# The last wait of a decode kernel: ahead of SyncE's final branch, or behind it

## The chip, the cores and the metric

The kernel runs on one core of a Trainium2 chip. The metric is the device time of one execution in microseconds (us). The profile lists the instructions of five engines apart: TensorE, called PE; VectorE, called DVE; ScalarE, called ACT; GpSimd, called POOL; SyncE, called SP. A "q" behind an engine's name in the profile (SPq) means its sequencer: waits, branches and issues of transfers. The profile's span runs from the first to the last instruction of the program; a little of the timed execution comes after it, and this case is about that part (in the profiled run of the kernel before, 1286.23 us were timed and the span is 1284.81 us).

"Landing" means here the last update that a finished transfer makes to its semaphore.

## The reference

One decode step: layer norm of a row `x` of 640 numbers, attention over a cache of 32 heads, 32,768 positions and 128 numbers per position, and beside it a SwiGLU block; both are added to `x`.

```python
def _A_ref(x, k_cache, v_cache, wq, wo):
    ...
    scores = jnp.einsum("bhqd,bhkd->bhqk", q, k) * (Dh ** -0.5)
    p = _softmax(scores, axis=-1)
    o = jnp.einsum("bhqk,bhkd->bhqd", p, v)
    return (...)(o, 0, 2, 1, 3).reshape(B, Sq, Hq * Dh) @ wo

def _B_ref(x, w_gate, w_up, w_down):
    return (_silu(x @ w_gate) * (x @ w_up)) @ w_down

xn = _layernorm(x, axis=-1)
return x + _A_ref(xn, ...) + _B_ref(xn, ...)
```

The K and V caches are bfloat16, 268 MB each. The output is one row of 640 bfloat16 numbers.

## The kernel before

SyncE issues nearly all transfers, in the order in which buffers come free. At the end it waits for the output row, issues the store, and waits until the store has landed. Each engine's function lies in a block; when the block closes, each engine gets a branch to a common final block. The kernel empties that final block, so nothing of the program follows the branch.

```python
        block = es.enter_context(nc.Block(no_gpsimd_drain=True))
        ...
            @block.sync
            def sp(e):
                ...                                   # K, V and weight loads
                e.wait_ge(s_fin, 2)                   # the output row is there
                e.dma_start(out[0, 0:1, :].rearrange("o (r m) -> (o r) m", m=32),
                            orow[:, :]).then_inc(s_out, 16)
                e.wait_ge(s_out, 16)                  # the store has landed
        ...
            @block.vector
            def dve(v):
                ...
                v.wait_ge(s_or, 1)
                v.tensor_copy(out=orow[:, :], in_=orow_ps).then_inc(s_fin, 1)

    nc.main_func.blocks[-1].instructions = []         # behind the exit from the block
```

Of the kernel before, what the change touches and what calls it, by code (L numbers as in the profile page):

```python
# [12 lines left out]
def bass_parallel_sum__gqa_block_cached__swiglu_ffn__decode_kernel(  # L13
# [66 lines left out]
    with ExitStack() as es:  # L80
# [3 lines left out]
        def sem(name):  # L84
            return es.enter_context(nc.semaphore(name))
# [34 lines left out]
        s_x, s_wq, s_out = sem("x"), sem("wq"), sem("o")  # L120
# [26 lines left out]
        def ahead(start):  # L147

            at_start = nc.main_func.blocks[0]
            n = len(at_start.instructions)  # L150
            start()
            ins = list(at_start.instructions)
            new = ins[n:]
            drain = next(i for i, x in enumerate(ins)
                         if x.engine == new[0].engine and type(x).__name__ == "InstDrain")
            at_start.instructions = ins[:drain] + new + ins[drain:n]

        ahead(lambda: nc.sync.dma_start(wq, A_wq.rearrange("(p c) n -> p (c n)", c=NCD)).then_inc(s_wq, 16))
        ahead(lambda: nc.scalar.dma_start(xrow, A_x[0, 0:1, :]).then_inc(s_x, 16))
        block = es.enter_context(nc.Block(no_gpsimd_drain=True))  # L160
        f0 = FFN_S * CE
        wg = flat[:, f0:f0 + NCD * F]
        wu = flat[:, f0 + NCD * F:f0 + 2 * NCD * F]
# [22 lines left out]
        def kv_src(cache, h, j0, n):  # L186
            return cache[0, h].rearrange("(p j) d -> p (j d)", p=128)[:, j0 * DH:(j0 + n) * DH]
# [20 lines left out]
        with nc.psum_tensor("ps8", [128, 8, 512], F32) as ps8:  # L208
# [11 lines left out]
            @block.sync  # L220
            def sp(e):
                owner = {}
                for u in units:
                    s = slot_of[u]
                    if s in owner:
                        e.wait_ge(*owner.pop(s))
                    if u[0] == "wq":
                        owner[s] = (s_q, NQB)
                    elif u[0] == "k":
                        e.dma_start(ring[:, s, :], kv_src(A_k_cache, u[1], 0, NJ)).then_inc(s_slot[s], 16)  # L230
                        owner[s] = (s_qk, NHF * (u[1] + 1))
                    elif u == LASTV:
                        j = 0
                        for i, n in enumerate(TAIL):
                            e.dma_start(ring[:, s, j * DH:(j + n) * DH],
                                        kv_src(A_v_cache, u[1], j, n)).then_inc(s_tail[i], 16)
                            j += n
                    elif u[0] == "v":
                        e.dma_start(ring[:, s, :], kv_src(A_v_cache, u[1], 0, NJ)).then_inc(s_slot[s], 16)
                        owner[s] = (s_pv, u[1] + 1)  # L240
                    elif u[0] == "ffn":
                        e.dma_start(wg, B_w_gate.rearrange("(p c) n -> p (c n)", c=NCD)).then_inc(s_ffn[0], 16)
                        e.dma_start(wu, B_w_up.rearrange("(p c) n -> p (c n)", c=NCD)).then_inc(s_ffn[1], 16)
                        e.dma_start(flat[:, d0:d0 + FM * D], B_w_down[0:FM * 128, :].rearrange(
                            "(p j) n -> p (j n)", j=FM)).then_inc(s_ffn[2], 16)
                        e.dma_start(wdr, B_w_down[FM * 128:F, :].rearrange(
                            "f (t n) -> (f t) n", t=2)).then_inc(s_ffn[2], 16)
                    else:
                        wo_src = A_wo.rearrange("(p j) n -> p (j n)", j=OC)
                        j = 0  # L250
                        for i, n in enumerate(WTAIL):
                            e.dma_start(wo[:, j * D:(j + n) * D], wo_src[:, j * D:(j + n) * D]).then_inc(s_wo[i], 16)  # L252
                            j += n
                e.wait_ge(s_fin, 2)
                e.dma_start(out[0, 0:1, :].rearrange("o (r m) -> (o r) m", m=32), orow[:, :]).then_inc(s_out, 16)
                e.wait_ge(s_out, 16)

            @block.gpsimd
            def pool(g):
# [383 lines left out]
                v.wait_ge(s_or, 1)  # L643
                v.tensor_copy(out=orow[:, :], in_=orow_ps).then_inc(s_fin, 1)

    nc.main_func.blocks[-1].instructions = []


# [26 lines left out]
```

## Time and profile before

| what | value |
|---|---|
| time, median of the first three runs | 1286.45 us (1286.17 to 1286.59) |
| span | 1284.8 us |
| mean transfer rate over the span | 431 GB/s |
| issue of the output store | 1283.50 us |
| landing of the store | 1284.756 us |
| end of the span | 1284.806 us |
| last update of the closing sequence | 1286.344 us |

The last four lines are counted from the span's start. The last landing and the last update come from the trace's records of semaphore updates, to the nanosecond; none of the views lists these. The semaphore of the store has eleven updates there: one 0.50 us after the start of its issue, then ten, 13 to 14 ns apart, the last of them at 1284.756.

First the page of the kernel before: its span, the transfers in 40 slices of it in tenths, and the shares of the chain that ended last.

```profile
span 1284.8 us, 10032 instructions
...
DMA  9999999999999999999999999999999999999998
...
DMA 53%; PE 29%; DVE 11%; issue 6%; DVEq 0%; SPq 0%
```

The transfer engines are busy for 9 tenths or more in 39 of the 40 slices; only the last falls below. With 554.16 MB moved at a mean of 431 GB/s, and 51% of the chain that ended last in transfers of K alone, the stream of K and V sets the time.

The timeline of the kernel before, from 1282.5 us (start, duration, engine, line, operation, output<-inputs; in brackets the idle time before it and what ended it):

```profile
1282.82 0.18 DVE L641 TENSOR_TENSOR outb<-ps,blk 128x20 bf16<-128x20 f32 x1 [11.11 <-PE ps L451]
...
1283.06 0.20 PE L476 MATMUL ps<-fold,outb 128*20 128x32 bf16 x1 [0.27 <-DVE outb L641]
1283.29 0.18 DVE L644 CAST orow<-ps 20x32 bf16<-20x32 f32 x1 [0.29 <-PE ps L476]
1283.50 0.39 SPq L255 DMA_DIRECT2D out_dram<-orow  x1
```

Then the waits of SyncE's queue (line that waited <- what it waited for: us in total, times, longest), and the view of the source line 80:

```profile
SPq L80 <- DMA out_dram<-orow: 0.9, 1, 0.9
```

```profile
L80 POOLq COMPARE_BRANCH  x1: 33/33/33, 4.5 to 4.5; - x1
L80 SPq COMPARE_BRANCH  x1: 33/33/33, 1284.8 to 1284.8; - x1
```

The wait for the store was written on line 256, but the profile has it on line 80, which is the `with` statement whose exit closes the block. The compiler let the branch itself carry the wait. So the order on SyncE is: issue the store, 0.9 us of waiting, then a branch of 33 ns, with which the span ends.

What follows is not in the views, but its traces are in the record of semaphore updates. Semaphore 2 has four updates from 1283.431 to 1283.622 us, which I put down to the other engines. Its next update comes at 1285.024, 218 ns after the branch; I take it for SyncE's, since SyncE is the only engine that is late. Then 226 other semaphores have one update each, from 1285.158 to 1285.755, and semaphore 2 has its last at 1286.344. I read this as a closing barrier, a reset of the semaphores and a second barrier, and call it so; the records show the updates and not their purpose, nor what puts them in. From SyncE's update to the last one it takes 1.32 us.

### The profile page before, as it was taken

The numbers are of one execution on the slowest core, as the hardware profiler recorded it, in microseconds if no ns is written. First come the engines' busy times: TensorE is split into PE (matmuls) and PEld (weight loads), VectorE is DVE, ScalarE is ACT, GpSimd is POOL, SyncE is SP. The second block draws the span as 40 slices with busy tenths as digits, with TensorE's granted clock in tenths as the row PEclk, the third lists the DMA queues.
The fourth block names the chain that finished last, engine by engine and source line by source line (L and its number), as shares of the span: only waits on it lengthen the run. The fifth ranks groups of instructions, "written<-read, shape, count | busy, mean of one in ns | idle before, by whom it ended". The sixth has DMA issues, their size and how long they took to land.

```text
span 1284.8 us, 10032 instructions
## 1 busy us (share of the span) xinstructions
PE 1043.2 (81%) x5160; PEld 261.3 (20%) x3240; DVE 672.2 (52%) x409; ACT 52.2 (4%) x139; POOL 2.6 (0%) x18
## 2 busy tenths in 40 slices
PE   3599777789777788778898887798788798778897
PEld 1021112221112221112221112221112221112227
DVE  0855665445664446664446664446654446654451
ACT  2000000000000000000000000000000000000000
POOL 0000000000000000000000000000000000000000
PEclk9799888898888999888998888998888998888995
DMA  9999999999999999999999999999999999999998
GB/s 424 424 453 425 426 427 445 428 433 441 431 433 426 445 428 433 439 433 426 433 445 428 431 431 441 428 433 445 428 431 426 445 428 433 439 433 431 428 429 368
DMA packets 10987, 554.16 MB, mean 431 GB/s; under 512 B 1247, under 2 KB 1504, under 8 KB 1760
## 3 DMA queue, kind: packets, MB, share of 16 engines
q1 hardware_dynamic: 10974, 554.00, 99.8%
q8 instruction: 9, 0.15, 0.0%
q14 instruction: 2, 0.02, 0.0%
q10 hardware_dynamic: 2, 0.00, 0.0%
HBM read 553.99 MB, written 0.00 MB: 431 GB/s over the span
## 4 chain that ended last, share of the span: by engine, by line
DMA 53%; PE 29%; DVE 11%; issue 6%; DVEq 0%; SPq 0%
DMA ring<-in_A_k_cache_dram 51%; PE ps L358 16%; DVE ring L577 11%; PE ps L310 10%; DMA ring<-in_A_wo_dram 2%; PE ps L342 1%; PE ps L329 1%; PE ps L400 0%; PE ps L394 0%; PE ps L388 0%; PE ps L451 0%; SPq L252 0%; DVEq L577 0%; DVE sc L583 0%; DVE pmax L589 0%
## 5 line engine op out<-in xcount | busy, mean ns | idle before, releaser
L577 DVE TENSOR_TENSOR ring<-ring,qb 128x8192 bf16<-128x8192 bf16 x128 | 557.8, 4420 | 314.8 <-DMA ring<-in_A_k_cache_dram 314.8
L310 PE MATMUL ps<-ring,ident 128*128 128x512 bf16 x1920 | 498.9, 419 | 0.0
L358 PE MATMUL ps<-ring,P 128*4 128x512 bf16 x1920 | 429.0, 379 | 0.0
L329 PE MATMUL ps<-ring,ident 128*128 128x512 bf16 x128 | 55.9, 437 | 218.7 <-DVE ring L577 218.2
L358 PEld LDWEIGHTS ps<-ring,P 128*4 128x4 bf16 x1920 | 158.1, 85 | 230.1
L329 PEld LDWEIGHTS ps<-ring,ident 128*128 128x128 bf16 x128 | 12.6, 99 | 616.9 <-issue 313.3
L583 DVE TENSOR_REDUCE sc<-ps 128x64 f32<-128x512 f32 x128 | 82.3, 684 | 63.8 <-PE ps L310 63.8
L595 DVE TENSOR_SCALAR negb<-ps 128x1 f32<-128x1 f32 x32 | 5.1, 159 | 108.4 <-PE ps L400 108.4
L503 ACT ACTIVATE P<-sc,negb 128x256 bf16<-128x256 f32 x32 | 16.2, 508 | 956.9 <-DVE negb L595 956.9
L592 DVE TENSOR_REDUCE m<-ps 1x1 f32<-1x128 f32 x32 | 8.9, 278 | 85.2 <-PE ps L394 85.2
L380 PEld LDWEIGHTS ps<-identf,o 4*128 4x128 f32 x248 | 30.7, 190 | 13.1 <-issue 13.1
L380 PE MATMUL ps<-identf,o 4*128 4x1 f32 x248 | 33.3, 251 | 0.0
L388 PEld LDWEIGHTS ps<-rsum,ones 128*128 128x128 f32 x64 | 12.1, 190 | 99.9 <-issue 99.1
L494 ACT ACTIVATE o<-ps,rzb 4x512 f32<-4x512 f32 x31 | 21.0, 678 | 6.3 <-PE ps L345 6.3
L301 PE MATMUL ps<-ring 128*128 x40 | 11.1, 448 | 10.6 <-DMA ring<-in_A_wq_dram 10.6
L499 ACT ACTIVATE ocol<-ps 128x1 f32 (+1 forms) x31 | 5.4, 174 | 222.3 <-PE ps L380 222.3
L342 PE MATMUL ps<-ring,P 128*4 x64 | 14.4, 379 | 0.0
L589 DVE TENSOR_REDUCE pmax<-sc 128x1 f32<-128x256 f32 x32 | 13.4, 420 | 0.0
L394 PE MATMUL ps<-identf,pmax 128*1 128x128 f32 x64 | 12.2, 272 | 1.2 <-DVE pmax L589 1.2
L400 PE MATMUL ps<-m,ones 1*128 1x1 f32 x64 | 12.1, 256 | 0.4 <-DVE m L592 0.4
L400 PEld LDWEIGHTS ps<-m,ones 1*128 1x128 f32 x64 | 9.4, 182 | 14.0 <-issue 13.3
L565 DVE RECIPROCAL rzb<-ps 128x1 f32<-128x1 f32 x32 | 5.1, 158 | 8.1 <-PE ps L388 8.1
(75 smaller groups left out, 97.4 us busy)
## 6 DMA issues: line engine op xcount, KB each, us to landing
ring<-in_A_v_cache_dram SPq DMA_DIRECT2D x2, 4096.0 KB, 36.3
ring<-in_A_wq_dram SPq DMA_DIRECT2D x1, 5120.0 KB, 15.0
ring<-in_A_wo_dram SPq DMA_DIRECT2D x3, 1280.0 KB, 24.2
ring<-in_B_w_gate_dram SPq DMA_DIRECT2D x1, 2160.0 KB, 22.6
ring<-in_B_w_up_dram SPq DMA_DIRECT2D x1, 2160.0 KB, 27.5
ring<-in_B_w_down_dram SPq DMA_DIRECT2D x1, 2080.0 KB, 30.9
ring<-in_A_wo_dram SPq DMA_DIRECT2D x1, 800.0 KB, 28.3
ring<-in_A_k_cache_dram SPq DMA_DIRECT2D x32, 41.4
```

The lines of the kernel that those rows point to most:

```text
L310: return t.add_instruction(mybir.InstMatmult(start_tensor_calc=False, stop_tensor_calc=stop, tile_size=(128, 128), tile_position=(0, 0), l ...
L329: t.matmul(ob, lhsT=ident[:, :], rhs=src, start=True, stop=False)
L342: t.matmul(O, lhsT=P[:, h % PR, bass.ds(b * (RUN * W) + j, W)], rhs=flat[:, bass.ds(b * (RUN * W * DH) + (s * CE + j * DH), W * DH)], star ...
L358: mm = t.matmul(O, lhsT=P[:, h % PR, j:j + W], rhs=ring[:, s, j * DH:(j + W) * DH], start=(j == 0), stop=(j + W == NJ))
L380: mm = t.matmul(fold_ps, lhsT=o4[:, m * DH:(m + 1) * DH], rhs=identf[0:W, m:m + 1], start=(m == 0), stop=(m == W - 1))
L394: t.matmul(misc[0:1, 0:128], lhsT=pmax[:, h % SR:h % SR + 1], rhs=identf[:, :], start=True, stop=True).then_inc(s_t, 1)
L400: t.matmul(misc[:, 128:129], lhsT=ones[0:1, :], rhs=m1[0:1, h % SR:h % SR + 1], start=True, stop=True).then_inc(s_b, 1)
L494: a.activation(out=o4[:, :], in_=O, func=ACTF.Copy, scale=rzb[0:W, h % SR:h % SR + 1]).then_inc(s_o4, 1)
L503: a.activation(out=P[:, h % PR, :], in_=sc[:, :], func=ACTF.Exp, bias=negb[:, h % SR:h % SR + 1], scale=c_scale, accum_out=rsum[:, h % SR: ...
L577: v.tensor_tensor(out=kh, in0=kh, in1=q[:, None, :].to_broadcast([128, HF, DH]), op=ALU.mult).then_inc(s_mul, 1)
L583: v.tensor_reduce(out=sc[:, i * HF:(i + 1) * HF], in_=bank[i].rearrange("p (j e) -> p j e", e=G), axis=AX.X, op=ALU.add).then_inc(s_red, 1)
L589: v.tensor_reduce(out=pmax[:, h % SR:h % SR + 1], in_=sc[:, :], axis=AX.X, op=ALU.max).then_inc(s_max, 1)
```

## The change

The intent: the branch (33 ns in the view above) costs time behind the landing, where nothing hides it. Taken first, it would run while the store is under way, and only the bare wait would be left for the end.

```diff
-        block = es.enter_context(nc.Block(no_gpsimd_drain=True))
+        body = ExitStack()
+        block = body.enter_context(nc.Block(no_gpsimd_drain=True))
...
                 e.dma_start(out[0, 0:1, :]..., orow[:, :]).then_inc(s_out, 16)
-                e.wait_ge(s_out, 16)
...
-    nc.main_func.blocks[-1].instructions = []
+        body.close()
+        nc.main_func.blocks[-1].instructions = []
+        nc.sync.wait_ge(s_out, 16)
```

## The prediction

> **What bounds the kernel.** The page of the profile gives a span of 1284.8 us, a DMA share of 9 tenths in 39 of 40 slices and a mean of 431 GB/s. The chain that ended last is 53% DMA and 29% PE. Nearly all of the time is the stream of K and V from HBM; the change does not touch it.
>
> **Where the change acts.** It acts after the last compute. The timeline's last entry is SyncE issuing the output store at 1283.50 us (0.39 us). The waits of the SyncE queue list one wait of 0.9 us for the store's landing, on the source line of the block's end: the view of that line shows one COMPARE_BRANCH of 33 ns on SyncE (start 1284.773), which carries the wait. So the order now is: issue, wait for landing, branch, end. The span ends with this branch, at 1284.806. The trace also records semaphore updates after it: 218 ns pass until SyncE's update of the closing barrier (1285.024), and the last closing update is at 1286.34, near the profiled run's 1286.23 us. So a closing sequence of about 1.5 us seems to be in the timed 1286.45 us, and it starts only when SyncE is through its branch. The other four engines had updated that barrier by 1283.62.
>
> **What the change removes, adds and moves.** It moves the branch into the 0.9 us in which SyncE waits anyway, and adds one bare semaphore wait in the final block (17 ns on SyncE elsewhere in the trace). The landing, 1.27 us from issue to wait's end, stays.
>
> What comes off the critical path is the branch (33 ns against 17 ns) and the restart of SyncE's instruction stream at the branch target, which has no record. Estimates: a taken loop branch on PE takes 208 ns, a not taken one 76 ns: 132 ns. From its last completed work to a barrier update PE needed about 160 ns and DVE about 140 ns; SyncE needed 268 ns from the landing's last recorded update (1284.756). The difference is about 0.1 us. [...] 218 ns leave no room for one, since instruction fetches in this trace take about 1 us per 16 KB packet. So I expect no saving of a microsecond.
>
> **Sum.** The gain is about 0.1 us (0.05 to 0.2), 0.01% of the time, under the 0.42 us spread of the three runs before. Predicted: 1286.35 us, range 1285.8 to 1286.8. Chances: faster by over 2% 0.002, within 2% 0.996, slower by over 2% 0.002.
>
> **What would show it right.** SyncE's wait for the store stays at about 0.9 us but on a semaphore instruction that ends the span; the COMPARE_BRANCH with the wait is gone; the span shortens by about 0.02 us or drowns in noise; SyncE's barrier update follows the landing by about 0.15 us, not 0.27; everything before 1283.5 us is the same.
>
> **What would make it wrong.** The runtime's ending waits for something else, so nothing starts earlier; the branch target needs a fetch that collides with the store; or the HBM stream differs between runs by more than the effect, which is likely at this size.

What is cut from it, for the reading of its sum: it came to a gain of about 0.1 us, so 1286.45 less 0.1 = 1286.35 us, and no term of that is gone. Cut are a figure for the time of a branch, which I had set beside the 0.1 us as a check, and a statement on when a branch waits for a fetch of instructions; no run here shows either. In what is left, "no room for one" means room for such a fetch. The "restart" of the stream was an assumption of mine with a size estimated from this trace, and "the runtime's ending" is my name for the closing sequence; neither is shown as such.

## The result, and the profile after

| | before | after |
|---|---|---|
| time, median of 4 runs each | 1286.36 us (1286.17 to 1286.59) | 1286.26 us (1286.17 to 1286.32) |
| ratio of after to before, 95% interval | | 0.9999 (0.9982 to 1.0016) |
| span of the profiled run | 1284.806 us | 1284.897 us |
| issue of the store | 1283.499 us | 1283.606 us |
| landing to SyncE's update of the barrier | 268 ns | 197 ns |
| landing to the last closing update | 1588 ns | 1515 ns |

A ratio is the mean time of one kernel's fast runs over that of the other's from the same rounds, so it isn't quite the ratio of the medians. By time alone the two kernels are the same. The last two lines show the effect of the change: 71 ns come off between the landing and the barrier, and they arrive at the end (73 ns).

The span of the changed kernel is 0.09 us longer, though its ending is shorter. In this execution the store was issued 0.107 us later; that comes from the stream ahead of it, not from the change: the matmuls on the last weights (line 451) already began 0.09 us later (1281.43 against 1281.34 us). The page, the timeline, the waits and the view of the last source line, of the kernel after:

```profile
span 1284.9 us, 10032 instructions
...
DMA  9999999999999999999999999999999999999998
```

```profile
1283.40 0.18 DVE L644 CAST orow<-ps 20x32 bf16<-20x32 f32 x1 [0.29 <-PE ps L476]
1283.61 0.39 SPq L256 DMA_DIRECT2D out_dram<-orow  x1
```

```profile
SPq L648 <- DMA out_dram<-orow: 0.9, 1, 0.9
```

```profile
L648 SPq EVENT_SEMAPHORE  x1: 17/17/17, 1284.9 to 1284.9; - x1
```

The wait is as long as before, 0.9 us, but a semaphore instruction of 17 ns carries it now, on the line that the change added. The trace has no SyncE branch in the block's exit any more.

Is it only unrecorded, or not there? The end of SyncE's compiled program settles it (one line per instruction; labels are marks for branch targets):

```text
before: DMA store | COMPARE_BRANCH, waits for the store | 19 labels
after:  DMA store | 19 labels | EVENT_SEMAPHORE, waits for the store
```

The compiled kernel before has 9 COMPARE_BRANCH instructions in all, the kernel after has 8. (Listing and counts are of the compiled programs; no view of the profile has them.) The final block follows directly in SyncE's program, so a branch to it with nothing to wait for does nothing, and the compiler drops it. **The change did not move the branch into the waiting time; it made it vanish.** The words of the change describe a program that was not built.

### The profile page after: what moved, and what is told of

The parts are those of the page before. It is cut to its first block, busy times and chain, and to the rows that moved or that the text cites. A ratio compares the mean times of both kernels' runs of the same rounds, so it can differ in the third digit from the quotient of the medians.

```text
span 1284.9 us, 10032 instructions
## 1 busy us (share of the span) xinstructions
PE 1042.9 (81%) x5160; PEld 261.2 (20%) x3240; DVE 672.2 (52%) x409; ACT 52.1 (4%) x139; POOL 2.6 (0%) x18
## 4 chain that ended last, share of the span: by engine, by line
DMA 53%; PE 29%; DVE 12%; issue 5%; SPq 0%; DVEq 0%
DMA ring<-in_A_k_cache_dram 51%; PE ps L358 16%; DVE ring L577 12%; PE ps L310 10%; DMA ring<-in_A_wo_dram 2%; PE ps L342 1%; PE ps L329 1%; PE ps L400 0%; PE ps L394 0%; PE ps L388 0%; PE ps L451 0%; SPq L253 0%; DVEq L577 0%; DVE sc L583 0%; DVE pmax L589 0%
```

## The experiments

All kernels gave correct results. "Landing to barrier" is read as above: from the last update of the store's semaphore to SyncE's update of the barrier. Every change described as "against after" or "against before" starts from that kernel. All clocks were 0.887 to 0.890, as before.

| run | what SyncE does behind the store's issue | landing to barrier, ns | landing to last update, ns |
|---|---|---|---|
| before, before_again | branch that carries the wait | 268, 268 | 1588, 1588 |
| after, after_again | wait alone | 197, 197 | 1515, 1514 |
| branch_ahead | branch, then wait | 201 | 1520 |
| wait_in_block | wait (in its old place), no branch | 213 | 1532 |
| wait_then_branch | wait, then branch | 378 | 1697 |
| hops_ahead6 | 7 branches, then wait | 742 | 2060 |
| sems_after | wait, 31 semaphore instructions | 2296 | 3609 |
| hops_after | wait on the first of 32 branches | 4775 | 6090 |
| far_after | wait on a far branch | 2606 | 4010 |
| far_ahead | far branch, then wait | 2041 | 3359 |

### before_again: is the 268 ns a property of the program?

No edit.

> The kernel before, profiled a second time. Measured: the interval from the last recorded update of the store's semaphore to SyncE's update of the closing barrier (semaphore 2), 268 ns in the first profile of before and 197 ns in that of after. If the 71 ns are an effect of the program, this run shows 268 ns within about 10 ns. If they are noise of one execution, it may show anything from 190 to 280 ns.

Measured: 268 ns, and 1588 ns to the end, both equal to the first profile to the nanosecond. This interval repeats far better than the time: the issue of the store, which the stream of K and V sets, lay between 1283.435 and 1283.876 us over all twelve profiles, 0.44 us apart. The difference of 71 ns is therefore a property of the program and not noise.

### branch_ahead: the change as its words have it

```diff
# against after
                 e.dma_start(out[0, 0:1, :]..., orow[:, :]).then_inc(s_out, 16)
+                e.wait_ge(s_fin, 2)      # already met; the branch carries it and is kept
```

> The change as its words say it: in the compiled program of after SyncE has no branch left at all, so here the branch gets a wait that is already met and is therefore kept, ahead of the wait for the store. Theory R (a taken branch behind the landing costs its 33 ns and a restart of the stream): a COMPARE_BRANCH is recorded before the landing and the interval landing to barrier is 197 ns, as in after. Rival D (only the missing branch helps, one branch less anywhere): the interval is near 268 ns.

The view of the two lines in question, of this run:

```profile
L647 SPq COMPARE_BRANCH  x1: 33/33/33, 1284.2 to 1284.2; - x1
```

```profile
L649 SPq EVENT_SEMAPHORE  x1: 17/17/17, 1284.7 to 1284.7; - x1
```

The branch is there and is taken at 1284.214 us, 0.48 us ahead of the landing at 1284.698. Landing to barrier is 201 ns. A branch that is really taken first is as good as none, to within 4 ns. Rival D, by which only a missing branch helps, falls.

### wait_in_block: does the place in the source matter?

```diff
# against before
                 e.wait_ge(s_out, 16)
+                e.sem_inc(s_fin, 1)      # this instruction carries the wait, so the branch doesn't
```

> The wait stays in the engine's own block, ahead of the branch in the source, but a semaphore instruction carries it, so that the compiler drops the branch. Theory R: 197 ns from landing to barrier, as in after, since no branch follows the landing. Rival P (it matters that the wait stands in the final block): 268 ns, as before.

Measured: 213 ns. The 16 ns above 197 lie behind the wait: in both runs the instruction that waits ends 34 ns after the landing, and the barrier update follows 179 ns later here, 163 ns in after. Two things differ there, the added count and the place of the 19 labels, which lie behind the wait here; this run does not separate them. The wait stands where it stood in the kernel before, and 55 of the 71 ns are still gained. So neither the final block nor the separate context for the block is needed; it is enough that no branch follows the landing. Rival P falls.

### wait_then_branch: is it the branch, or the wait that it carries?

```diff
# against before
                 e.wait_ge(s_out, 16)
+                e.sem_inc(s_fin, 1)
+                e.wait_ge(s_fin, 2)      # already met; the branch carries it
```

> A semaphore instruction carries the wait for the store, and a branch with a wait that is already met follows it. Theory R: the branch and its restart are still behind the landing: 268 ns plus about 17 ns for the added instruction, so 270 to 300 ns. Rival C (a wait that a branch carries is answered later than one on a semaphore instruction, and a branch itself is cheap): 197 ns plus 17 to 33 ns, so 215 to 235 ns.

Measured: 378 ns, outside both expectations. The record shows why: the wait ends 34 ns after the landing and the branch begins only 92 ns later. I had counted 17 ns for one more instruction and left out the gap between two instructions of SyncE; together, 109 ns, they make up the 110 ns by which 378 exceeds 268. The question itself is answered by what follows the branch: 219 ns from its end to the barrier, against 218 ns in the kernel before. A branch that waits and one that doesn't are followed by the same gap, and it is 55 ns longer than the 163 ns behind a bare wait. Rival C also had a wait on a branch answered late; but the branch of before starts 17 ns after the landing, and so does the semaphore instruction of after. Rival C falls.

So the 71 ns are accounted for: 16 ns because a branch takes 33 ns where the bare wait takes 17, and 55 ns because the barrier update comes later behind the branch (218 ns) than behind the bare wait (163 ns). That SyncE's stream resumes later because the branch is taken is theory R's name for these 55 ns. No run has a branch in this place that is not taken, so it is not shown whether the jump or the branch instruction as such costs them. They are no wait for a fetch: the last instruction fetch started 114 ns after SyncE's update in before and 126 ns ahead of it in before_again, where it was still under way at the update, and the interval was 268 ns both times.

### hops_after and sems_after: thirty-two times as much

```diff
# hops_after, against before
                 e.wait_ge(s_out, 16)
+                for n in range(32):
+                    e.wait_ge(s_fin, 2)          # already met
+                    e.br(f"hop{n}")
+                    nc.switch_bb(f"hop{n}")

# sems_after, against before
                 e.wait_ge(s_out, 16)
+                e.sem_inc(s_fin, 1)
+                for n in range(31):
+                    e.wait_ge(s_fin, 2)          # already met
+                    e.sem_inc(s_fin, 1)
```

> 32 taken branches behind the landing in place of 1 (each carries a wait that is already met, so that it is kept; each goes to the next instruction). Measured so far: one more semaphore instruction behind the landing cost 110 ns (378 against 268), and a branch in its place cost 71 ns more than a semaphore instruction (268 against 197). Theory R (a taken branch costs a restart of the stream): each hop takes about 110 + 71 = 180 ns, so the interval landing to barrier is about 268 + 31 x 180 = 5.8 us (4.5 to 7), the time rises by about 5.6 us, and hops_after is about 2.2 us slower than sems_after. Rival S (every SyncE instruction costs the same and a branch has no cost of its own): about 31 x 110 = 3.4 us more, the same as in sems_after.

> The control of hops_after: 32 semaphore instructions behind the landing (the first carries the wait for the store, the others waits that are already met; each also counts one semaphore up), and no branch. Both theories: about 31 x 110 = 3.4 us more than the 213 ns of the run with one such instruction, so 3.6 us (2 to 4). Theory R: about 2.2 us less than hops_after; rival S: the same as hops_after.

The time was 1290.83 us for hops_after and 1288.23 us for sems_after, with 1286.27 us for the kernel before in the same rounds; ratios 1.0036 (1.0019 to 1.0052) and 1.0015 (0.9998 to 1.0032). The two groups in the view of their line, one fence for each run:

```profile
L259 SPq COMPARE_BRANCH  x32: 32/33/33, 1284.9 to 1289.4; - x32
```

```profile
L260 SPq EVENT_SEMAPHORE  x31: 17/17/17, 1285.0 to 1287.0; - x31
```

Thirty-two branches take 4.5 us from the first to the last, and 31 semaphore instructions 2.0 us. In the records the steady step is 145 ns from branch to branch and about 67 ns from one semaphore instruction to the next. A taken branch therefore costs 78 ns more than a semaphore instruction, near the 71 ns of the change. (Behind the last of each chain the barrier update follows 203 and 133 ns later, both less than behind a single instruction, but again 70 ns apart.) The step of both was smaller than I expected (180 and 110 ns), because I had taken the gap behind the first wait, 92 ns, for the steady one, which is 50 ns. The difference that separates the theories is 2.6 us in time (1290.83 less 1288.23) and 2.48 us from landing to barrier (4775 less 2296), against 2.2 expected by theory R and none by rival S. Rival S falls.

These runs also show that the timed execution contains what follows the span. The times rose by 4.56 and 1.96 us over the kernel before; the interval from landing to last update rose by 4.50 (6090 less 1588) and 2.02 us (3609 less 1588). In far_after, below, most of the added time is outside the span: the profiled run took 1288.98 us, with a span of 1285.1 us.

### hops_ahead6: how much fits ahead of the landing

```diff
# against after
                 e.dma_start(out[0, 0:1, :]..., orow[:, :]).then_inc(s_out, 16)
+                for n in range(6):
+                    e.wait_ge(s_fin, 2)
+                    e.br(f"hop{n}")
+                    nc.switch_bb(f"hop{n}")
+                e.wait_ge(s_fin, 2)
```

> Seven taken branches ahead of the wait for the store, which stands in the final block. Measured so far: 145 ns from one such branch to the next, and the first of them started 0.39 us after the end of the store's issue, 0.48 us ahead of the landing. So three of them are hidden and the seventh ends 0.39 + 6 x 0.145 + 0.03 = 1.3 us after the issue's end, 0.42 us after the landing, and the wait itself some 0.1 us later. If hiding ends where the landing wait ends, the interval landing to barrier is 0.6 to 0.8 us. If any number of branches ahead of the wait were free, it would be 197 ns.

```profile
L259 SPq COMPARE_BRANCH  x6: 33/33/33, 1284.3 to 1285.0; - x6
```

Six of the branches are in this group, the seventh follows at 1285.187; the store had landed at 1284.777. The interval is 742 ns, within the expectation. Work ahead of the wait is free only until the landing. The room was smaller than the 0.9 us wait of the profile: with a wait (already met) right behind the issue, the first branch began 0.40 us after the issue had ended (0.39 us in branch_ahead).

### far_after and far_ahead: a target 1024 instructions away

```diff
# both: a test that is never true jumps over 1024 instructions
+                zero_r = e.alloc_register("never")   # at the start of SyncE's function
+                e.reg_mov(zero_r, 0)
...
                 # far_after: e.wait_ge(s_out, 16) stands here; far_ahead: only in the final block
+                with e.If_ne(zero_r, 0):
+                    for _ in range(1024):
+                        e.sem_inc(s_fin, 1)
```

> The branch that carries the wait for the store now jumps over 1024 instructions that are never run[...]. Theory F (a branch to code that is not fetched waits for a fetch): the interval landing to barrier grows from 268 ns by about 0.8 us, to 0.7 to 1.6 us, and an instruction fetch starts after the branch; the last fetch in the profiles of before and after took 0.3 to 0.5 us for its data alone. Rival (targets cost the same near or far): 268 ns.

> The same jump over 1024 instructions, but ahead of the wait, which stands in the final block: what the change's words describe, with a branch that really is there. In the run with a kept branch SyncE took that branch 0.48 us ahead of the landing. If a fetch takes 0.8 us from there, 0.3 us of it are left behind the landing: an interval of 0.2 to 0.6 us, and 0.4 to 0.6 us less than far_after, in the timed runs too. If the fetch starts earlier or is shorter: 197 ns, all hidden. If position doesn't matter: as far_after.

Measured: 1288.80 us for far_after and 1287.99 us for far_ahead, against 1286.27 us for the kernel before; ratios 1.0019 (1.0002 to 1.0036) and 1.0013 (0.9996 to 1.0029). The branch of far_ahead and the wait behind it, in the views of their lines:

```profile
L259 SPq COMPARE_BRANCH  x1: 45/45/45, 1284.0 to 1284.0; - x1
```

```profile
L653 SPq EVENT_SEMAPHORE  x1: 17/17/17, 1286.7 to 1286.7; - x1
```

The branch ends at 1284.062 us and the next instruction starts at 1286.708: 2.65 us for one jump. The store had landed at 1284.828, so 0.77 us of the jump were hidden and the rest was not. In far_after all of it lies behind the landing: 2544 ns from the branch's end to the barrier, against 218 ns for the near branch. The rival (near or far cost the same) falls. Theory F fits as far as a fetch does follow the jump; that the jump waits for it is not shown, and both sizes were wrong: for far_after I expected 0.8 us and the jump adds 2.34 us (2606 less 268); for far_ahead I expected an interval of 0.2 to 0.6 us and it is 2.04. I had only the transfer of the instructions to go by (0.3 to 0.5 us), and the 0.8 us of a fetch was an estimate. In the trace the fetch that follows the jump starts 0.87 us after the branch and takes 0.40 us (0.87 and 0.57 us in far_ahead); what the rest of the 2.5 us consists of the trace does not show. Nor does a run have the same register test with only a few instructions to jump over, so the share of the test itself is untested on SyncE. The nine loop branches of ScalarE in the kernel before (line 516) are register tests too, of 40 to 45 ns, and the next instruction follows each of them within 0.31 us.

The queue of these fetches, first of the kernel before and then of far_ahead (packets, MB, share):

```profile
q14 instruction: 2, 0.02, 0.0%
```

```profile
q14 instruction: 4, 0.03, 0.0%
```

Of the two packets more, one came at 1262.75 us, 21 us before the jump; the other, at 1284.936, is the fetch behind it. In far_after that fetch lies behind the end of the span. The branch of far_ahead, which carries no wait, began 0.06 us after the end of the store's issue.

Putting the far branch ahead of the wait gained 0.57 us from landing to barrier (2606 less 2041, within the 0.4 to 0.6 expected), 0.65 us from landing to last update (4010 less 3359) and 0.81 us in time. Not all of the last figure is the branch: the two profiled executions differ by 0.91 us, and 0.26 us of that is a later issue of the store in far_after. That is the change's idea at work, and eight to nine times its effect here.

### after_again: the time once more

No edit.

> The changed kernel, once more, beside the kernel before in five rounds. Its trace: 197 ns from landing to barrier within 5 ns, and about 1515 ns from the landing to the last closing update (before: 268 and 1588, twice). Its time: the two traces say 0.07 us less than before. The executions of before spread over about 0.45 us, so the medians should lie within 0.2 us of each other, and the interval of the ratio will not be able to tell 0.07 us from nothing.

Measured: 1286.17 us (1286.10 to 1286.31, five runs) against 1286.31 us (1286.22 to 1286.89, nine runs); ratio 0.9998, interval 0.9985 to 1.0012. The trace again has 197 ns, and 1514 ns to the last update. The timed difference of 0.14 us has the right sign and is no proof; the interval is 50 times wider than 0.07 us of 1286. The evidence for the gain is the interval in the traces.

## Why the prediction was right or wrong, point by point

- *The time, 1286.35 us, and "same".* Right: 1286.26 us. It would have been right for any gain from 0 to 0.5 us, so it proves little.
- *Where the change acts: "A closing sequence of about 1.5 us seems to be in the timed 1286.45 us, and it starts only when SyncE is through its branch."* Right. The profiled time was 0.11 to 0.12 us less than the last closing update in eleven of the twelve profiles, over a range of 5 us; in before_again it was 0.03 us less (1286.44 against 1286.468). So the timed interval contains that sequence.
- *The gain, "about 0.1 us (0.05 to 0.2)".* Right in where it lies, somewhat large: 0.071 us. The instruction itself (33 against 17 ns) was in the prediction, and what it called the restart, put at the remaining part of about 0.1 us, is 55 ns; that these 55 ns are a restart is not shown.
- *"It moves the branch into the 0.9 us in which SyncE waits anyway."* Wrong. The compiler dropped the branch, and nothing moved. branch_ahead shows that a moved branch would have given the same to within 4 ns, so the number survived; that was luck, since nothing in the prediction had weighed a branch that vanishes. The hint was there before: in the profile the branches of PE, DVE and ACT to the final block, which carry no wait, had no record either, while GpSimd's, which carries a wait, has one (the first line of the view of line 80). I read that as "no record" and should have asked whether they exist.
- *No fetch behind the branch: "218 ns leave no room for one".* Right, and the far jump fits it: with a target 1024 instructions away, and a fetch behind the jump, the 218 ns become 2544. The reason given looked at the wrong queue: the 16 KB packets of about 1 us are those of q8, while the fetch behind the far jump came on q14 (8 KB; 0.40 and 0.57 us). Even the shortest packet of that size in the trace of before, 0.31 us, is longer than 218 ns, so the conclusion stands.
- *What the profile would show.* The wait of 0.9 us on a semaphore instruction that ends the span: right. The COMPARE_BRANCH gone: right. The barrier update 0.15 us after the landing instead of 0.27: it was 0.197. The span 0.02 us shorter "or drowned in noise": drowned, it was 0.09 longer. "Everything before 1283.5 us is the same": not to 0.1 us, since the store was issued 0.107 us later.
- *What an instruction of SyncE costs.* The prediction and the first expectations used the 17 ns of the record. The step between two of them is 67 ns, and was 104 to 109 ns directly behind the wait that ended. This did no harm to the prediction, where one instruction replaced another, but it did to the expectation of wait_then_branch.

## What to carry to other kernels

What stood behind the last wait of this program was paid in full (32 semaphore instructions in place of the one branch raised the time by 1.96 us, 32 branches by 4.56 us), so let the last instruction be a bare wait and put branches and bookkeeping ahead of it. A near branch was worth 0.07 us here, which the timings of this 1286 us kernel did not resolve, while moving the far branch ahead of a 0.9 us wait was worth 0.57 us; so look at where the target lies before spending work on it. A branch with a wait on it is a real instruction and one without may not exist (9 COMPARE_BRANCH in the compiled kernel before, 8 after), so before explaining a moved instruction check that it is in the compiled program; and for effects this small compare an interval between two events in the trace, which repeated within a nanosecond, not the total, which scattered by 0.4 us.
